# Linear attention feeding a Swish MLP: input weights and first V as fp32 on the hardware DMA queue, cast on chip; first queries issued by two engines

## The chip, the cores and the metric

The kernel runs on one core of a Trainium2 chip. The metric is the device time of one execution in microseconds (us); lower is better. The kernel before took 290.16 us (median of three runs, 289.76 to 290.47). Engines: PE is TensorE's matmuls and PEld its weight loads, DVE is VectorE, ACT is ScalarE, POOL is GpSimd, SP is SyncE. SP, ACT and POOL can all issue DMAs. SP and ACT use the hardware queue (q1 and q10 in the profile), POOL the software queue (q0).

All runs quoted here count as "fast" (none more than 1.5% above the fastest of its kernel), so they can be compared.

## The reference, cut to what matters

```
q, k, v: [8 batches, 8 heads, 576, 64] fp32
q_s = softmax(q, over the 64);  k_s = softmax(k, over the 576)
attn = q_s @ (k_s^T @ v)                      # per batch and head
x = attn as [4608 tokens, 512]
h = x @ w_in                                   # 512 -> 2048
out = (h / (1 + exp(-beta*h))) @ w_out         # 2048 -> 512
```

## The kernel before

The tokens are worked off in nine slabs of 512. Slabs 0 to 7 are the first 512 positions of one batch each; the last slab holds the rests. A slab's pass 1 is `h` for 16 blocks of 128 columns (four matmuls each, then one Swish activation on ACT, which writes `GT`); pass 2 is `@ w_out`. Attention of the next batches is threaded between those matmuls at fixed "slots". Only the first two batches are special: batch 0's attention runs in front (the *head*), and batch 1's is squeezed into slab 0's pass 2, because its inputs have just come. The product `k_s^T @ v` is called the kv product below; a query pair is the queries of two of the eight heads.

The parts that matter here:

```
# batch 0's loads, all issued by SyncE, in this order
load_main("qf", qt_h, QF, 0, 4)        # queries: four loads of 256 KB
load_k(0, 4)                           # K: four loads of 288 KB
... (beta)
# V of batch 0 and the input weights: GpSimd's DMA, which casts fp32 to bf16 on the way
def load_vb(hp):                       # two of these, 0.59 MB read each
    add(POOL, lambda e: e.dma_start(o, a), ..., after=P.writer[("qf", 0, 2)])
def load_win(c):                       # five of these, 4.19 MB read in all
    add(POOL, lambda e: e.dma_start(WIN[:, :, c0:c0 + n], a), ...)
    if c == 2:
        wgate.append(P.ops[-1])        # the output weights may be issued when this has landed
...
load_vb(0)
warm(8, 0)                             # filler matmuls that keep PE busy
exp_q(0); exp_kh(...)                  # ACT: exponentials
norm_main(0, 0, 1)                     # DVE: sum, reciprocal, multiply
norm_main(0, 1, 1, POOL)               # the multiply of query pair 1 on GpSimd
...
# slab 0, pass 2: loads for batch 1 follow the output weights (1 MB each)
for c in range(4): load_wout(c)
...
for cs in ((0, 1), (2, 3)):
    load_main("qf", qt_h, QF, 1, 4, cs)
    load_k(1, 4, cs)
load_v(1, 4)                           # four loads of 288 KB, cast to bf16 by GpSimd
```

The weight columns of block `f` are not neighbours: PE's weight load takes 128 columns with a step of `n`, and the rows of `w_out` are read in the matching order, so that they come in longer pieces. `n` is 2 for `f < 4` and 4 from there on.

The softmax here doesn't subtract the row's maximum and nothing guards it: scores larger than these inputs give would overflow.

## Time and profile before

| what | number | view |
|---|---|---|
| time | 290.16 us, profiled run 290.93 | runs |
| span, PE busy | 289.1 us, 96% | the page |
| dense pass 1 of slab 0 begins | 18.1 to 19.8 us | timeline |
| PE waits for batch 1's V in slab 0 | weight loads 1.3 us, in two waits | waits |
| from slab 1's first activation to the end | 235.92 us | timeline |

The page of the kernel before, its first lines and its chain of waits (part 4, followed back from the last instruction):

```profile
span 289.1 us, 3841 instructions
PE 278.7 (96%) x1566; PEld 137.8 (48%) x1597; DVE 111.4 (39%) x199; ACT 176.8 (61%) x237; POOL 38.1 (13%) x58
...
q1 hardware_dynamic: 37738, 43.92, 50.0%
q0 software_dynamic: 3184, 2.69, 6.3%
...
PE 82%; DMA 7%; SPq 5%; POOL 3%; issue 2%; DVE 0%; POOLq 0%
```

PE is the bottleneck nearly everywhere, so only what makes PE wait can be won. The queue lines give packets and megabytes as they are *written*: the 5.37 MB of fp32 that the software queue read count as 2.69, because it writes bf16.

The timeline of the head (start us, length us, engine, line, operation, output<-input; in brackets the idle time before it and what ended it):

```profile
0.74 2.00 SPq L254 DMA_DIRECT2D QF<-in_q_dram  x4
...
3.43 0.63 ACT L297 ACTIVATE EQ<-QF 128x512 bf16<-128x512 f32 x1 [1.20 <-DMA QF<-in_q_dram]
...
7.77 0.63 ACT L297 ACTIVATE EQ<-QF 128x512 bf16<-128x512 f32 x1 [0.67 <-DMA QF<-in_q_dram]
7.77 1.04 POOL L336 TENSOR_TENSOR EQ<-EQ,QI 128x512 bf16<-128x512 bf16 x1
8.09 1.27 DVE L336 TENSOR_TENSOR EQ<-EQ,QI 128x512 bf16<-128x512 bf16 x1
```

The last of the four query loads is used at 7.77 us. GpSimd's multiply also starts there, beside a VectorE multiply that takes 1.27 us (alone it takes 0.69).

The timeline of slab 0, where batch 1's V comes in:

```profile
44.05 0.88 POOL L353 CAST VB<-VF 128x576 bf16<-128x576 f32 x1 [3.13 <-DMA VF<-in_v_dram]
...
44.98 0.10 PEld L367 LDWEIGHTS PS<-VB,EK 128*128 128x128 bf16 x1 [0.98 <-POOL VB L353]
...
45.14 0.67 POOL L353 CAST VB<-VF 128x576 bf16<-128x576 f32 x1 [0.21 <-DMA VF<-in_v_dram]
...
45.86 0.10 PEld L367 LDWEIGHTS PS<-VB,EK 128*128 128x128 bf16 x1 [0.33 <-POOL VB L353]
...
53.18 1.26 ACT L649 ACTIVATE GT<-PS,BETA 128x512 bf16<-128x512 f32 x2 [0.48 <-PE PS L367]
```

GpSimd waits for a load, PE waits for GpSimd. The last line is slab 1's first activation.

Two stretches in the windows view (stretch, its length, busy us of PE, PEld, DVE, ACT and POOL with instruction counts, granted PE clock, DMA share, GB/s written):

```profile
2.00:6.00 4.00, 2.89 (x9) 0.90 (x8) 1.84 (x4) 1.48 (x4) 2.50 (x5) 1.00 0.95 290
10.00:22.00 12.00, 11.21 (x109) 6.77 (x110) 5.34 (x17) 7.13 (x11) 5.94 (x10) 1.00 1.19 174
```

The first is queries and K on the hardware queue. The second is almost all software queue; 174 GB/s written as bf16 are 348 GB/s read as fp32.

### The profile page before, as it was taken

The page shows a single profiled execution, that of the slowest core. Times are in us where ns is not written, and L with a number is a line of the kernel's source. Part 1 is how long each engine was busy: PE and PEld are TensorE (multiplying, and loading weights), DVE is VectorE, ACT ScalarE, POOL GpSimd, SP SyncE. Part 2 cuts the span into 40 slices and gives each one's busy share as a digit, 9 for nine tenths or more (in the row PEclk, how much of TensorE's full clock was granted, in tenths as well). Part 3 has the DMA queues.
Part 4 walks back from the last instruction along what each step waited for, and adds up shares of the span by engine and source line. Part 5 has one row for each costly group of instructions (what it writes and reads, how often), then busy time and mean ns, then how long its engine had stood idle before and what let it go on. Part 6 is the DMA issues. An engine that isn't in the chain of part 4 may idle for free.

```text
span 289.1 us, 3841 instructions
## 1 busy us (share of the span) xinstructions
PE 278.7 (96%) x1566; PEld 137.8 (48%) x1597; DVE 111.4 (39%) x199; ACT 176.8 (61%) x237; POOL 38.1 (13%) x58
## 2 busy tenths in 40 slices
PE   6899998999999999999999999999999999999994
PEld 2455444454555444544454445544544454445441
DVE  4641667206883147304660555054804300110021
ACT  4748774879987963788378926892660076018500
POOL 5920014022603011300040000000000000000000
PEclk9999999999999999999999999999999999999999
DMA  6999999995699999905990025001800030012022
GB/s 215 198 193 346 405 376 302 356 384 146 162 381 240 347 325 403 126 0 168 384 194 0 2 91 128 2 1 51 170 17 0 0 147 0 0 67 80 0 74 73
DMA packets 41260, 47.38 MB, mean 164 GB/s; under 512 B 20117, under 2 KB 31383, under 8 KB 39834
## 3 DMA queue, kind: packets, MB, share of 16 engines
q1 hardware_dynamic: 37738, 43.92, 50.0%
q0 software_dynamic: 3184, 2.69, 6.3%
q10 hardware_dynamic: 320, 0.52, 0.5%
q8 instruction: 12, 0.20, 0.3%
q14 instruction: 6, 0.05, 0.0%
HBM read 36.71 MB, written 9.44 MB: 160 GB/s over the span
## 4 chain that ended last, share of the span: by engine, by line
PE 82%; DMA 7%; SPq 5%; POOL 3%; issue 2%; DVE 0%; POOLq 0%
PE PS L367 82%; DMA VF<-in_v_dram 4%; DMA WIN<-in_moe_w_in_dram 3%; SPq L254 3%; SPq L264 1%; POOL EK L238 1%; SPq L548 1%; POOL VB L602 1%; POOL WIN L564 1%; POOL EQ L336 0%; DVE O2S L701 0%; POOL VB L353 0%; POOL IDB L226 0%; PE PS L365 0%; POOL KVD L241 0%
## 5 line engine op out<-in xcount | busy, mean ns | idle before, releaser
L649 ACT ACTIVATE GT<-PS,BETA 128x512 bf16<-128x512 f32 x144 | 98.1, 687 | 79.2 <-PE PS L367 79.0
L367 PE MATMUL PS<-WOUT,GT 128*128 128x512 bf16 x562 | 131.8, 379 | 0.6
L367 PE MATMUL PS<-XT,WIN 128*128 128x512 bf16 x561 | 131.1, 380 | 1.0 <-ACT XT L526 0.3
L367 PEld LDWEIGHTS PS<-XT,WIN 128*128 128x128 bf16 x576 | 62.2, 109 | 59.6 <-DVE XT L526 1.5
L367 PEld LDWEIGHTS PS<-WOUT,GT 128*128 128x128 bf16 x576 | 54.5, 98 | 62.1 <-DVE O2S L701 0.2
L701 DVE COPY O2S<-PS 128x512 f32<-128x512 f32 x34 | 23.2, 686 | 110.7 <-PE PS L367 110.7
L367 PE MATMUL PS<-VB,EK 128*128 128x65 bf16 (+1 forms) x288 | 36.6, 198 | 1.1 <-POOL VB L353 0.7
L353 POOL CAST VB<-VF 128x576 bf16<-128x576 f32 x28 | 20.0, 713 | 74.6 <-PE PS L367 60.6
L309 ACT ACTIVATE EK<-KF 64x1152 bf16<-64x1152 f32 x24 | 27.8, 1158 | 0.4
L367 PEld LDWEIGHTS PS<-VB,EK 128*128 128x128 bf16 x288 | 22.8, 102 | 9.0 <-POOL VB L353 1.3
L334 DVE TENSOR_REDUCE QS<-EQ 128x8 f32<-128x512 bf16 (+1 forms) x22 | 20.2, 919 | 3.3 <-ACT EQ L297 3.1
L297 ACT ACTIVATE EQ<-QF 128x512 bf16<-128x512 f32 x32 | 18.0, 620 | 5.2 <-DMA QF<-in_q_dram 5.0
L442 DVE CAST XT<-PS 128x512 bf16<-128x512 f32 x24 | 16.4, 690 | 10.9 <-PE PS L367 10.9
L336 DVE TENSOR_TENSOR EQ<-EQ,QI 128x1024 bf16<-128x1024 bf16 (+1 forms) x16 | 17.4, 1085 | 0.6
L367 PE MATMUL PS<-QT,KVD 128*128 128x512 bf16 x31 | 11.6, 379 | 0.2
L336 POOL TENSOR_TENSOR EQ<-EQ,QI 128x512 bf16<-128x512 bf16 x6 | 6.2, 1040 | 34.2 <-DVE QI L335 33.9
L319 ACT ACTIVATE EK<-KF 64x1152 bf16<-64x1152 f32 (+1 forms) x10 | 9.5, 966 | 1.8 <-DMA KF<-in_k_dram 1.6
L367 PE MATMUL PS<-WARM 128*128 128x512 bf16 x18 | 8.9, 631 | 1.4 <-DVE ONE L223 1.2
L404 DVE TENSOR_TENSOR KVD<-PS,RC 64x128 bf16<-64x128 f32 (+1 forms) x22 | 7.7, 349 | 2.9 <-PE PS L367 2.3
L342 DVE TENSOR_REDUCE QRS<-EQR 128x8 f32<-128x512 bf16 x4 | 2.7, 680 | 14.4 <-ACT EQR L324 14.4
L526 ACT CAST XT<-PS 128x512 bf16<-128x512 f32 x4 | 2.2, 587 | 7.6 <-PE PS L367 7.6
L553 DVE TENSOR_SCALAR WOUT<-WST,RB 128x512 bf16<-128x512 f32 x8 | 3.3, 483 | 8.5 <-DMA WST<-in_moe_w_out_dram 8.5
(48 smaller groups left out, 82.6 us busy)
## 6 DMA issues: line engine op xcount, KB each, us to landing
out_dram<-O2S SPq DMA_DIRECT2D x8, 1024.0 KB, 5.5
KF<-in_k_dram SPq DMA_DIRECT2D x6, 1152.0 KB, 9.6
VF<-in_v_dram SPq DMA_DIRECT2D x6, 1152.0 KB, 11.2
QF<-in_q_dram SPq DMA_DIRECT2D x6, 1024.0 KB, 7.5
KF<-in_k_dram SPq DMA_DIRECT2D x8, 288.0 KB, 7.3
QF<-in_q_dram SPq DMA_DIRECT2D x8, 256.0 KB, 8.8
WST<-in_moe_w_out_dram SPq DMA_DIRECT2D x2, 1024.0 KB, 8.7
O2S<-in_moe_w_out_dram SPq DMA_DIRECT2D x2, 1024.0 KB, 12.7
```

The costliest lines, as they stand in the source:

```text
L254: add(SP, lambda e, c=c: e.dma_start(dst(bufs[i], c * n, n), src(th, b, c * n, n)), w=[(name, i, hp) for hp in range(c * n // 2, (c + 1) * ...
L297: add(ACTE, lambda e, o=o, a=a: e.activation(o, a, ACT.Exp), r=[("qf", i, hp)], w=[("eq", i, hp)])
L309: add(ACTE, lambda e, o=o, a=a: e.activation(o, a, ACT.Exp), r=[("kf", i, h) for h in hps], w=[("ek", i, h, e_) for h in hps])
L319: add(ACTE, lambda e: e.activation(o, a, ACT.Exp), r=[("kf", i, h) for h in hps], w=[("ek", i, h, e_) for h in hps])
L334: add(DVE, lambda e: e.tensor_reduce(s_, a, AX.X, ALU.add), r=ks, w=[("qs", i, hp0)])
L336: add(eng, lambda e: e.tensor_tensor(a, a, vb, ALU.mult), r=ks + [("qi", i, hp0)], w=ks)
L353: add(eng, lambda e: (e.copy if eng == ACTE else e.tensor_copy)(o, a), r=[("vf", i, h) for h in hps] + [("vone", i)], w=[("vb", i, h) for ...
L367: add(PE, lambda e: e.matmul(o, l, r_, start=start, stop=stop), r=r, w=w, bank=[bk])
L404: add(DVE, lambda e, o=o, a=a, s_=s_: e.tensor_tensor(o, a, s_, ALU.mult), r=[("ps", bk)] + [("rc", i, h) for h in hps], w=[("kvd", i, h, ...
L442: add(eng, lambda e: (e.copy if eng == ACTE else e.tensor_copy)(XT[i][:, hp, :], PS[bk][:, :]), r=[("ps", bk)], w=[("xt", i, hp)], bank=[bk])
L649: add(ACTE, lambda e: e.activation(GT[:, f, :], PS[bk][:, :], ACT.Silu, scale=BETA[:, f:f + 1]), r=[("ps", bk), "beta"], w=[("gt", f)], ba ...
L701: add(eng, lambda e: (e.copy if eng == ACTE else e.tensor_copy)(O2S[t % 2][:, u, :], PS[bk][:, :]), r=[("ps", bk)], w=[("o2", t % 2, u)], ...
```

## The change

The intent: no DMA from GpSimd. V of batch 0 and the input weights are loaded as fp32 through SyncE, into buffers that the output weights use later, and cast on GpSimd (V, columns 0 to 511), ScalarE (a quarter of V) and VectorE (columns 512 to 2047). GpSimd is then free sooner. Batch 0's four query loads are issued by SyncE and ScalarE in turn. Along with that, columns 512 to 1023 change their step from 4 to 2, and one group of transposes moves by two slots. The cut diff leaves out what follows from this: batch 0's V gets the padded layout of the other batches with a column of ones, which K's sums now multiply by instead of the constant `ONE`, and the output weights wait for the casts that free their buffers instead of the gate `wgate`.

```diff
-FG = {2: (0, 256), 4: (512, 1024, 1536)}
-WCH = ((0, 256), (256, 256), (512, 512), (1024, 512), (1536, 512))
+FG = {2: (0, 256, 512, 768), 4: (1024, 1536)}
+WCH = ((0, 256), (256, 256), (512, 256), (768, 256), (1024, 512), (1536, 512))
...
-        load_main("qf", qt_h, QF, 0, 4)
+        load_main("qf", qt_h, QF, 0, 4, None, (SP, ACTE))
...
+        load_v(0, 4)
...
         def load_win(c):
-            add(POOL, lambda e, c0=c0, n=n, a=a: e.dma_start(WIN[:, :, c0:c0 + n], a),
-                w=[("win", c)], slot=f"win{c}")
-            if c == 2:
-                wgate.append(P.ops[-1])
+            s = STAGE[c0 // 512][:, :, c0 % 512:c0 % 512 + n]
+            add(SP, lambda e: e.dma_start(s, a), w=ks, slot=f"win{c}")
+        def cast_win(c, m, nm, eng):
+            add(eng, lambda e: e.tensor_copy(WIN[:, x, c0:c0 + n], s), r=ks, ...)
...
-        load_vb(0)
...
+        for hp in range(3):
+            cast_v(0, hp)
+        for m in range(NM):
+            cast_win(0, m, 1, POOL)
+        for m in range(0, NM, 2):
+            cast_win(1, m, 2, POOL)
...
+        cast_v(0, 3, ACTE)
...
-            n = 2 if f < 4 else 4
+            n = 2 if f < 8 else 4
...
-        TT = (104, 119)
+        TT = (106, 119)
...
+        for c in range(2, len(WCH)):
+            for m in range(0, NM, 2 if c < 4 else 1):
+                cast_win(c, m, 2 if c < 4 else 1, DVE)
```

More of the change, by code (lines that the diff above doesn't have):

```diff
@@ L210, in bass_efficient_attn_shen__then__act_swish_beta_kernel @@
         DUMMY = sb("DUMMY", [128, 8], F32)
-        ONE = sb("ONE", [128, 2], BF16)
         PS = [es.enter_context(nc.psum_tensor(f"PS{i}", [128, 512], F32)) for i in range(8)]
@@ L222, in bass_efficient_attn_shen__then__act_swish_beta_kernel @@
         add(DVE, lambda e: e.memset(WARM[:, :], 0.0), w=["warm"])
-        add(DVE, lambda e: e.memset(ONE[:, :], 1.0), w=["one"])
         add(POOL, lambda e: e.iota(IOTA[:, :], [[1, 128]], base=0, channel_multiplier=-1,
@@ L229, in bass_efficient_attn_shen__then__act_swish_beta_kernel @@
             r=["iota"], w=["idf"])
-        def v_ones(i):
-            add(POOL, lambda e: e.memset(VB[i][:, :, :, D:VW], 1.0),
-                w=[("vone", i)] + [("vb", i, hp) for hp in range(NHP)])
         def homes(i):
+            add(POOL, lambda e: e.memset(VB[i][:, :, :, D:VW], 1.0), w=[("vone", i)])
             for e_ in range(2):
@@ L248, in dst, with load_main @@
             return bass.AP(t, h0 * 4 * D, [[H * 4 * D, 128], [4 * D, nh], [1, 4 * D]])
-        def load_main(name, th, bufs, b, split=1, cs=None):
+        def load_main(name, th, bufs, b, split=1, cs=None, engs=(SP,)):
             i = b % 2
@@ L253, in load_main @@
             for c in cs or range(split):
-                add(SP, lambda e, c=c: e.dma_start(dst(bufs[i], c * n, n), src(th, b, c * n, n)),
+                add(engs[c % len(engs)], lambda e, c=c: e.dma_start(dst(bufs[i], c * n, n), src(th, b, c * n, n)),
                     w=[(name, i, hp) for hp in range(c * n // 2, (c + 1) * n // 2)],
@@ L506, in ksum @@
             for j in range(NG):
-                l, _, ke, _, _ = kv_rows(b, hp, j)
-                mm(PS[kb][:, hp:hp + 1], l, ONE[:, 0:1], j == 0, j == NG - 1, r=ke + ["one"],
+                l, r_, ke, kv, ko = kv_rows(b, hp, j)
+                mm(PS[kb][:, hp:hp + 1], l, r_[:, D:D + 1], j == 0, j == NG - 1, r=ke + ko,
                    w=[("ps", kb)], bk=kb)
@@ L517, in kv_mm @@
             for j in range(NG):
-                l, _, ke, kv, _ = kv_rows(b, hp, j)
-                r_ = bass.AP(VB[0], hp * KW + j * D, [[NHP * NG * VW, 128], [1, D]])
-                mm(PS[bk][:, VW * n:VW * n + D], l, r_, j == 0, j == NG - 1,
+                l, r_, ke, kv, ko = kv_rows(b, hp, j)
+                mm(PS[bk][:, VW * n:VW * n + D], l, r_[:, 0:D], j == 0, j == NG - 1,
                    r=ke + kv, w=[("ps", bk)], bk=bk)
@@ L539, in bass_efficient_attn_shen__then__act_swish_beta_kernel @@
                 slot=f"bt{i}")
+        load_v(0, 4)
         STAGE = (WST[0], WST[1], O2S[1], O2S[0])
-        SKEY = ([("wst", 0)], [("wst", 1)], [("o2", 1, u) for u in range(4)],
+        SKEY = ([("wst", 0), ("wst", 2)], [("wst", 1), ("wst", 3)], [("o2", 1, u) for u in range(4)],
                 [("o2", 0, u) for u in range(4)])
         def load_wout(c):
-            n = 2 if c == 0 else 4
+            n = 2 if c < 2 else 4
             a = bass.AP(wout_h, 512 * c * DM, [[n * DM, 128], [128 * n * DM, 4 // n], [1, n * DM]])
@@ L548, in load_wout @@
             add(SP, lambda e: e.dma_start(o, a), w=SKEY[c],
-                slot=f"wst{c}", after=wgate if c == 0 else ())
+                slot=f"wst{c}")
         def scale_wout(c):
@@ L558, in bass_efficient_attn_shen__then__act_swish_beta_kernel @@
         HEAD = (1, 2, 3, 4, 5, 6, 7)
-        wgate = []
         def load_win(c):
@@ L563, in load_win @@
             a = bass.AP(win_h, c0, [[DFF, 128], [128 * DFF, NM], [1, n]])
-            add(POOL, lambda e, c0=c0, n=n, a=a: e.dma_start(WIN[:, :, c0:c0 + n], a),
-                w=[("win", c)], slot=f"win{c}")
-            if c == 2:
-                wgate.append(P.ops[-1])
+            s = STAGE[c0 // 512][:, :, c0 % 512:c0 % 512 + n]
+            ks = SKEY[c // 2][c % 2:c % 2 + 1] if c < 4 else SKEY[c - 2]
+            add(SP, lambda e: e.dma_start(s, a), w=ks, slot=f"win{c}")
+        def cast_win(c, m, nm, eng):
+            c0, n = WCH[c]
+            x = m if nm == 1 else slice(m, m + nm)
+            s = STAGE[c0 // 512][:, x, c0 % 512:c0 % 512 + n]
+            ks = SKEY[c // 2][c % 2:c % 2 + 1] if c < 4 else SKEY[c - 2]
+            add(eng, lambda e: e.tensor_copy(WIN[:, x, c0:c0 + n], s), r=ks,
+                w=[("win", c, y) for y in range(m, m + nm)])
         def turn_beta():
@@ L597, in bass_efficient_attn_shen__then__act_swish_beta_kernel @@
         kb = bank(HEAD)
-        def load_vb(hp):
-            a = bass.AP(vt_h, hp * 2 * HS, [[KW, 128], [2 * HS, 2], [1, KW]])
-            o = bass.AP(VB[0], hp * KW, [[NHP * NG * VW, 128], [KW, 2], [1, KW]])
-            add(POOL, lambda e: e.dma_start(o, a), w=[("vb", 0, hp), ("vb", 0, hp + 1)],
-                slot=f"vb{hp}", after=P.writer[("qf", 0, 2)])
-        load_vb(0)
         warm(8, 0)
@@ L619, in bass_efficient_attn_shen__then__act_swish_beta_kernel @@
         norm_main(0, 3, 1)
-        load_vb(2)
         for c in range(len(WCH)):
             load_win(c)
+        for hp in range(3):
[4 more added lines that the diff above has]
+            cast_win(1, m, 2, POOL)
         homes(1)
-        v_ones(1)
         go(t_steps(0, (1,), HEAD))
@@ L641, in pass1_mm @@
             rd = [("xt8", p_) for p_ in range(4)] if t == 8 else [("xt", t % 2, m)]
-            n = 2 if f < 4 else 4
+            n = 2 if f < 8 else 4
             l = bass.AP(WIN, m * DFF + 128 * (f // n * n) + f % n, [[NM * DFF, 128], [n, 128]])
             mm(PS[bk][:, :], l, x[:, m, :], m == 0, m == NM - 1,
-               r=rd + [("win", c) for c in range(len(WCH))
+               r=rd + [("win", c, m) for c in range(len(WCH))
                        if WCH[c][0] <= 128 * (f // n * n) < WCH[c][0] + WCH[c][1]],
@@ L765, in bass_efficient_attn_shen__then__act_swish_beta_kernel @@
             elif t == 1:
-                v_ones(0)
                 for hp in range(NHP):
```

## The prediction

> **What bounds it now.** The page gives PE 96% of a 289.1 us span; the chain of waits is 82% PE matmuls. By stretch (the windows view), PE is busy 230.9 of the last 236.1 us. So two places can move the time: the head, until the dense pass-1 matmuls begin at 18.1 to 19.8 us (timeline), and the first slab, where the waits view has PE waiting some 1.3 us (44.5 to 46 us) for GpSimd's casts of V of batch 1. Behind those the chain runs over V loads, SyncE issues, and the input-weight load landing at 20.45 us that gates the output-weight loads. DMA share is 1.0 or more from 7 to 53 us: the V wait is a bandwidth wait.
>
> **What the change removes.** Seven GpSimd DMA issues (5.6 us of GpSimd), one of which held up GpSimd's multiply of query pair 1 until 7.77 us, its input ready at 6.58; and 5.37 MB read through the software queue from about 8.9 to 27 us, roughly 295 GB/s. The hardware queue in this trace moved 360 to 395 GB/s for Q, K and V, 430 for output weights. Estimate from these: 5.37 MB takes 14.5 us instead of 18.
>
> **What it adds.** GpSimd: three V casts at 0.67 to 0.88 us, input-weight casts of about 2.7 us by the same rate. ScalarE: one V cast, about 0.6, two query issues at about 0.5. VectorE: 12 casts of 128x512, at most 0.48 each as the output-weight scaling takes, so 4 to 6 us, where it is idle (20.4 to 28.1). The Trainium skill's GPSIMD Engine Reference (Key points) says GpSimd shares its SBUF interfaces with VectorE; this trace agrees: a VectorE multiply beside GpSimd's took 1.27 us, alone 0.69.
>
> **On the critical path.** Head: pair 1's multiply ends about 1 us sooner, pair 2's 0.5. But the K sums need ScalarE's exponentials (fourth K one ends at 11.07 us, sums start at 11.5), which follow K landings at 8.5 to 10.6; those hardly move. V should land at 11.4 to 13.5, casts end by 14.2, first input weights be cast by 16.3, before PE needs them (kv at 14.5, pass 1 at 17.7). Head gain 0.3 to 0.9 us. Issuing queries on two engines alone gains little: the queue was 0.94 busy from 2 us.
> Middle: output weights land 1 us sooner (first near 27 instead of 28.1), V of batch 1 near 42.8 instead of 44.0. PE gets there 0.5 us sooner, so its wait shrinks by about 0.7.
> Sum: about 1.1 us gained. Predicted 289.0 us, range 287.8 to 290.6; faster by over 2%: 1%, within: 95%, slower: 4%.
>
> **What would show it.** First pass-1 matmul near 17.6; no software queue in the DMA table; output weights landing near 27; V of batch 1 near 42.8, PE's wait for its casts under 1 us; the late stretch unchanged. Wrong if PE's wait in the head is for a V or weight cast.
>
> **What would make it wrong.** Staging is used twice: output weights cannot be issued before the input weights in their buffer are cast. If VectorE's casts end later than about 27 us, the queue runs dry and V of batch 1 comes later. Weight rows in 1 KB pieces may run no faster than the 285 to 297 GB/s of the first queries; VectorE casts may be late for input columns 512 to 1023, wanted at 22.5 us; two queues may delay the first query or K. The moved transposes (slot 106) hint that batch 1's queries may come later relative to PE.

## The result, and the profile after

The changed kernel took 289.12 us (median of four runs, 289.09 to 289.28); the kernel before took 289.96 us beside it. The ratio is 0.997, 95% interval 0.9953 to 0.9987. A ratio here is the mean time of one kernel's fast runs over that of the other's in the same rounds, so it is not quite the ratio of the medians. The interval leaves out 1. The predicted number, 289.0, was right within 0.12 us; how much of that was luck is told below.

The profile also looked like the prediction. The page after:

```profile
span 287.3 us, 3906 instructions
PE 279.0 (97%) x1597; PEld 136.0 (47%) x1597; DVE 114.7 (40%) x210; ACT 177.1 (62%) x238; POOL 38.5 (13%) x60
...
q1 hardware_dynamic: 41068, 48.77, 54.3%
q10 hardware_dynamic: 864, 1.05, 1.1%
...
PE 92%; DMA 3%; SPq 2%; POOL 2%; issue 0%; DVE 0%; POOLq 0%
```

The software queue is gone. The head and the place of batch 1's V, timeline:

```profile
0.75 1.04 ACTq L249 DMA_DIRECT2D QF<-in_q_dram  x2
0.75 0.98 SPq L249 DMA_DIRECT2D QF<-in_q_dram  x2
...
4.17 1.15 ACT L292 ACTIVATE EQ<-QF 128x512 bf16<-128x512 f32 x2 [0.85 <-DMA QF<-in_q_dram]
...
5.53 1.15 ACT L292 ACTIVATE EQ<-QF 128x512 bf16<-128x512 f32 x2 [0.21 <-DMA QF<-in_q_dram]
...
7.47 1.04 POOL L331 TENSOR_TENSOR EQ<-EQ,QI 128x512 bf16<-128x512 bf16 x1 [2.52 <-DVE QI L330]
...
8.47 0.69 DVE L331 TENSOR_TENSOR EQ<-EQ,QI 128x512 bf16<-128x512 bf16 x1
...
41.98 0.66 POOL L348 CAST VB<-VF 128x576 bf16<-128x576 f32 x1 [1.40 <-DMA VF<-in_v_dram]
...
43.63 0.10 PEld L362 LDWEIGHTS PS<-VB,EK 128*128 128x128 bf16 x1
...
51.66 0.69 ACT L648 ACTIVATE GT<-PS,BETA 128x512 bf16<-128x512 f32 x1 [0.48 <-PE PS L362]
```

V of batch 1 is cast 2.07 us sooner (41.98 against 44.05), and PE no longer waits for it. Slab 1 begins 1.52 us sooner.

The windows after, same stretches:

```profile
2.00:6.00 4.00, 2.79 (x7) 0.73 (x5) 1.10 (x3) 2.93 (x5) 2.67 (x6) 1.00 0.99 322
10.00:22.00 12.00, 11.48 (x112) 6.51 (x110) 6.60 (x20) 7.18 (x11) 7.93 (x14) 0.77 1.07 371
```

The clock column (1.00 before, 0.77 after, from 10 to 22 us) is not a difference between the kernels. The trace of before holds no clock record until 17.06 us, and the view counts that as 1.00; its filler matmuls at 12.80 and 13.22 us began 0.42 us apart, those of the trace after at 12.41 and 12.84 us 0.43.

It is tempting to stop here. But the two spans differ by 1.8 us where the medians differ by 0.8: the profile of before is of one of its slower runs. A single pair of traces cannot say which of the differences belong to the change. The experiments can.

A caution on the chain of waits. In the trace after, it runs from the input-weight load over GpSimd's casts and a GpSimd memset of `EK` to PE at 19.9 us. That memset clears batch 1's buffer, which those PE matmuls don't read. What they need, the third query-output cast on VectorE, ended at 19.13 us, and PE went on at 19.25. A wait with several semaphores is put down to the one that came last, here the wrong one.

### The profile page after: what moved, and what is told of

It is laid out like the page before. It is cut to its first block, busy times and chain, and to the rows that moved or that the text cites. A ratio compares the mean times of both kernels' runs of the same rounds, so it can differ in the third digit from the quotient of the medians.

```text
span 287.3 us, 3906 instructions
## 1 busy us (share of the span) xinstructions
PE 279.0 (97%) x1597; PEld 136.0 (47%) x1597; DVE 114.7 (40%) x210; ACT 177.1 (62%) x238; POOL 38.5 (13%) x60
## 4 chain that ended last, share of the span: by engine, by line
PE 92%; DMA 3%; SPq 2%; POOL 2%; issue 0%; DVE 0%; POOLq 0%
PE PS L362 91%; DMA WST<-in_moe_w_in_dram 3%; SPq L259 1%; POOL WIN L568 1%; POOL EK L233 1%; SPq L249 0%; PE PS L360 0%; DVE O2S L703 0%; SPq L532 0%; POOL VB L230 0%; POOLq L142 0%
## 5 line engine op out<-in xcount | busy, mean ns | idle before, releaser
L362 PE MATMUL PS<-WOUT,GT 128*128 128x512 bf16 x576 | 133.3, 379 | 0.0
L362 PEld LDWEIGHTS PS<-XT,WIN 128*128 128x128 bf16 x576 | 60.0, 106 | 60.7 <-POOL EK L233 0.7
L362 PE MATMUL PS<-VB,EK 128*128 128x65 bf16 (+2 forms) x324 | 37.1, 193 | 0.0
L348 POOL CAST VB<-VF 128x576 bf16<-128x576 f32 x31 | 22.5, 727 | 75.0 <-DMA VF<-in_v_dram 46.7
L362 PEld LDWEIGHTS PS<-VB,EK 128*128 128x128 bf16 x324 | 23.4, 100 | 8.0 <-issue 1.1
L331 DVE TENSOR_TENSOR EQ<-EQ,QI 128x1024 bf16<-128x1024 bf16 (+1 forms) x16 | 16.6, 1036 | 0.6
```

What stands on the lines that cost most here:

```text
L331: add(eng, lambda e: e.tensor_tensor(a, a, vb, ALU.mult), r=ks + [("qi", i, hp0)], w=ks)
L348: add(eng, lambda e: (e.copy if eng == ACTE else e.tensor_copy)(o, a), r=[("vf", i, h) for h in hps] + [("vone", i)], w=[("vb", i, h) for ...
L362: add(PE, lambda e: e.matmul(o, l, r_, start=start, stop=stop), r=r, w=w, bank=[bk])
```

## The experiments

Twelve kernels ran, each five rounds against the kernel before (six fast runs of each kernel). Each also left one trace, so there are 14 traces with the first two. The landings quoted are the last of a load's 16 completions in the trace's DMA records.

### First call: which part carries the gain?

The theory at this point was the prediction's: the hardware queue brings weights and V sooner, and GpSimd's freed second shortens the head. The rival: the query split does it.

**q_only.** The kernel before, with the split alone.

```diff
-        load_main("qf", qt_h, QF, 0, 4)
+        load_main("qf", qt_h, QF, 0, 4, None, (SP, ACTE))
```

> The kernel before with one part of the change alone: batch 0's query loads issued by SyncE and ScalarE in turn. Main theory (the gain is GpSimd's freed second in the head plus the faster landing of weights and V): this part alone gives nothing, 289.7 to 290.4 us, ratio 0.999 to 1.002; the first query lands later (near 4.1 instead of 3.4 us), the last one earlier (near 6.0 to 6.5 instead of 7.75), and the first dense pass-1 matmul stays within 0.3 us of 19.75. Rival (the query split is what helped): at least half of the measured 0.85 us, so 289.5 us or less.

Measured: 289.34 us (288.67 to 289.79), ratio 0.9978 (0.9948 to 1.0008). The median lies where the rival put it, not where the main theory did. The interval just includes 1.

**no_q.** The changed kernel with the split undone (the reverse of that diff).

> The changed kernel with the query split undone (all four loads from SyncE). Main theory: 288.8 to 289.3 us, the whole gain is kept; the first query lands near 3.4 us again. Rival (query split): it falls back by at least 0.4 us, to 289.5 or more.

Measured: 289.80 us (289.33 to 290.77), ratio 0.9999 (0.9968 to 1.0031). Again the rival's side: with all of the hardware queue and all casts in place, but not the split, the gain is gone.

**w_hw.** The kernel before with the input weights moved as in the change (loads on SyncE, casts, column order), V of batch 0 left on GpSimd's queue, queries left on SyncE.

```diff
-            add(POOL, lambda e, ...: e.dma_start(WIN[:, :, c0:c0 + n], a), ...)
+            add(SP, lambda e: e.dma_start(s, a), ...)      # and cast_win as in the change
```

> The kernel before with only the input weights moved to the hardware queue and cast on GpSimd and VectorE; V of batch 0 stays on GpSimd's DMA queue, queries stay on SyncE. Main theory: the head keeps its length (pair 1's multiply still near 7.8 us, first dense pass-1 matmul near 19.75, perhaps later if V now shares the engines with the weights), but output weights land near 27 to 27.6 us and V of batch 1 near 42, so PE's wait for its casts goes from about 1.3 us to under 0.5: 289.3 to 289.9 us. Rival (only the head counts, or only the query split): 290.0 or more.

Measured: 290.24 us, ratio 1.0008 (0.9978 to 1.0037). A miss for the main theory. The first output weights landed at 28.31 us, not near 27, and V of batch 1 at 43.5; PE's weight loads waited 1.2 us for its casts. In the head PE now also waited 1.5 us for batch 0's V, which shared the engines with the weights, as had been allowed for. So this kernel tells less than it should: it adds a wait of its own.

**mul_first.** The kernel before; GpSimd multiplies first and issues its first V load after that.

```diff
-        load_vb(0)
         warm(8, 0)
...
         norm_main(0, 1, 1, POOL)
+        load_vb(0)
```

> The kernel before with one reordering: GpSimd does pair 1's multiply before it issues the first V load. Main theory (the DMA issue held up the multiply, and the overlap of the two multiplies slowed VectorE): multiply at about 6.6 instead of 7.8 us, VectorE's pair-2 multiply near 0.69 instead of 1.27 us, PE's kv products start 0.3 to 0.5 us sooner unless V, issued a microsecond later, lands too late (its first half landed at 12.4, needed at 14.5); the wait for V of batch 1 then grows by what the head gains, because it is bound by DMA, so the time falls by 0.0 to 0.3 us only: 289.6 to 290.2. Rival (the head alone makes the gain): 289.4 or less.

Measured: 290.11 us, ratio 1.0000 (0.9965 to 1.0034). The mechanism was as expected: GpSimd's multiply at 6.80 us, VectorE's at its full speed (0.69 us), the first kv product at 14.24 instead of 14.93. The time did not move. Input weights then came later, and PE waited 1.6 us for them in slab 0.

### Second call: the method's own noise, and the column order

**before_again** and **after_again** are the two kernels unchanged.

> The kernel before, unchanged: a control for the method and a second trace. Ratio 1.000 within its interval; runs spread over 1 to 3 us. In the trace: the last K chunk of batch 0 lands between 10.2 and 10.7 us, V of batch 1 (first, second quarter) not before 42.8 and 43.9, as in all four traces without the query split (42.8 to 44.0); the stretch from the first activation of slab 1 to the end is 235.9 us, as in all traces of this column order.

> The changed kernel, unchanged: control and second trace, in the same rounds as the kernel before. Ratio 0.995 to 0.999. Query-split theory: last K chunk near 9.2 to 9.7 us, V of batch 1 near 41.9 and 43.0, as in both traces with the split. The stretch from slab 1's first activation to the end 235.65 us.

Measured: before_again 289.64 us (289.07 to 290.71), ratio 0.9982 (0.9954 to 1.0011); after_again 289.05 us (288.89 to 289.75), ratio 0.9959 (0.9936 to 0.9982). Two things follow. First, the same kernel can come out at 0.998 of itself, 0.5 us: differences of that size between two labels say nothing alone. Second, my marker fell. In this trace of the *kernel before*, batch 1's V landed at 41.61 and 42.52 us, sooner than in the changed kernel (41.92 and 43.30). The expectation had said "not before 42.8". The landing at the end of this long queue of loads varies by more than 2 us from run to run.

What separates the two groups in every trace is its beginning. In all seven traces without the split the last query landed between 6.61 and 7.75 us, in all seven with it between 5.69 and 6.02; and from 2 to 6 us the queues wrote 281 to 304 GB/s without, 322 to 336 with. The same window of three more kernels: q_only, no_q2 (the changed kernel without the split) and before_again:

```profile
2.00:6.00 4.00, 2.41 (x7) 0.76 (x5) 1.35 (x3) 2.94 (x5) 2.72 (x6) 1.00 1.04 327
```

```profile
2.00:6.00 4.00, 2.87 (x9) 0.87 (x8) 1.81 (x4) 2.05 (x5) 2.67 (x6) 1.00 0.95 304
```

```profile
2.00:6.00 4.00, 2.66 (x7) 0.73 (x5) 1.63 (x4) 1.67 (x5) 2.51 (x5) 1.00 0.91 288
10.00:22.00 12.00, 11.05 (x110) 6.44 (x112) 4.71 (x16) 6.99 (x11) 5.28 (x9) 0.81 1.24 188
```

A narrower window settles two rivals. From 3.5 to 4.8 us every data packet in all 14 traces is a 1 KB piece of a query: the query issues were over by 2.76 us, and K's first piece (2,304 bytes) started at 4.81 us or later. There the windows view gives 213 to 319 GB/s in the seven traces without the split and 360 to 381 in the seven with it. So in this stretch neither the issue time that SyncE saves nor K's larger pieces make the difference.

The last line shown is the software queue's stretch in before_again: 188 GB/s written, 376 read, against 371 for the hardware queue in the changed kernel. Over all traces with one of the two queues alone in this stretch, the software queue read 348 to 376 GB/s (six traces, mean 363) and the hardware queue 369 to 373 (seven). The two queues deliver nearly the same: by these rates the 5.37 MB take an estimated 14.8 and 14.5 us. The landings agree: from the last K load of batch 0 to column 1535 of the input weights, the same 4.33 MB (V and three quarters of the weights) took 12.3 and 12.4 us in the two traces of before and 12.7 and 12.0 us in the two of the changed kernel.

**fg_only.** The kernel before with the column order alone.

```diff
-FG = {2: (0, 256), 4: (512, 1024, 1536)}
+FG = {2: (0, 256, 512, 768), 4: (1024, 1536)}
-            n = 2 if f < 4 else 4
+            n = 2 if f < 8 else 4
```

> The kernel before with only the column order of weights 512 to 1023 changed from steps of 4 to steps of 2 columns (and the output weights' row order that goes with it). Column-order theory, from the four slabs' rates (257.2 against 254.2 ns per matmul of columns 512 to 1023 in slabs 2 to 6): the stretch from slab 1's first activation to the end is 235.65 instead of 235.92 us, slabs 2 to 6 show 254.2 ns; head and slab 0 as before; in time -0.25 us, which the rounds cannot tell from nothing (289.5 to 290.3). Rival (that stretch differs because of the moved slot or the V layout): it stays 235.9 and 257.2.

Measured: 289.87 us, ratio 0.9981 (0.9954 to 1.0008), as expected not to be told from nothing by the clock. But the trace tells it: the stretch from slab 1's first activation to the end is 235.66 us. That stretch is remarkably steady: 235.92 to 235.95 in the four traces with the old order, 235.64 to 235.67 in the ten with the new one. In slabs 2 to 6 a pass-1 matmul of columns 512 to 1023, with the short kv products that stand between, takes 254.2 instead of 257.2 ns (from the distances of the activations). The page's weight-load line for all pass-1 products has 109 ns per load in before and 106 in fg_only. In slabs 7 and 8, where no kv products stand between, the same columns take 215.8 to 215.9 ns in both orders: the step costs only where the short products are. The start of four activations of slab 2, before:

```profile
85.78 0.69 ACT L649 ACTIVATE GT<-PS,BETA 128x512 bf16<-128x512 f32 x1 [0.34 <-PE PS L367]
86.81 0.69 ACT L649 ACTIVATE GT<-PS,BETA 128x512 bf16<-128x512 f32 x1 [0.34 <-PE PS L367]
87.83 0.69 ACT L649 ACTIVATE GT<-PS,BETA 128x512 bf16<-128x512 f32 x1 [0.34 <-PE PS L367]
88.86 0.69 ACT L649 ACTIVATE GT<-PS,BETA 128x512 bf16<-128x512 f32 x1 [0.34 <-PE PS L367]
```

and in fg_only:

```profile
84.81 0.69 ACT L649 ACTIVATE GT<-PS,BETA 128x512 bf16<-128x512 f32 x1 [0.33 <-PE PS L367]
85.83 0.69 ACT L649 ACTIVATE GT<-PS,BETA 128x512 bf16<-128x512 f32 x1 [0.33 <-PE PS L367]
86.85 0.69 ACT L649 ACTIVATE GT<-PS,BETA 128x512 bf16<-128x512 f32 x1 [0.33 <-PE PS L367]
```

Three distances in the first fence make 3.08 us, two in the second 2.04: about 1.027 against 1.02 us per block. Small, but in every slab from 2 to 6.

**n1.** The changed kernel with step 1 for columns 0 to 1023.

```diff
-FG = {2: (0, 256, 512, 768), 4: (1024, 1536)}
+FG = {1: tuple(range(0, 1024, 128)), 4: (1024, 1536)}
-            n = 2 if f < 8 else 4
+            n = 1 if f < 8 else 4
```

> The changed kernel with columns 0 to 1023 in their natural order (step 1 instead of 2). If the step of the weight load is what costs where short kv products stand between, columns 512 to 1023 fall below 254.2 ns per matmul in slabs 2 to 6 and columns 0 to 511 below 241.3, the stretch from slab 1 to the end by some 0.3 us more, to about 235.3. Against it: output-weight rows are then read in 2 KB instead of 4 KB pieces, which may land them 0.2 to 0.6 us later. Time 288.6 to 289.4. Rival (the step does not matter below 4): 254.2 and 235.65 stay.

Measured: 289.54 us, ratio 0.9969 (0.9945 to 0.9994). The late stretch stayed at 235.65 us and the columns at 254.2 ns: step 4 costs, step 2 does not. The rival holds. The first output weights landed at 28.16 us in this trace, against 27.64 and 27.14 in the changed kernel, as feared, so there was nothing to win here.

### Third call: sufficient, necessary, and what bounds slab 0

**split_fg.** The kernel before with the split and the column order, nothing else.

> The kernel before with two small parts of the change only: the query split and the new column order. Input weights and V stay on GpSimd's DMA queue; no casts on GpSimd, VectorE or ScalarE are added. Theory now: the split is worth about 0.6 us, the order 0.27, the move to the hardware queue nothing, so this has the whole gain: 288.9 to 289.4 us, ratio 0.995 to 0.998, last query of batch 0 near 5.9 us, tail after slab 1's first activation 235.65. The prediction's theory (the hardware queue makes the gain): no more than the column order's 0.3 us, 289.6 or more.

Measured: 289.41 us (288.61 to 290.14), ratio 0.9978 (0.9951 to 1.0005). This is at the edge of what was expected, and three of its six runs were at 289.9 or more. The prediction's theory had put it at 289.6 or more. The point estimate favours the two small parts, but the run does not settle that they have the whole gain. Its trace shows where the software queue can still hurt: the head was short (first activation at 18.25 us, because the full clock came early, at 10.56), and PE's weight loads then waited 2.1 us in slab 0 for input weights, 1.17 of it for columns 512 to 1023 (landed at 20.79; at 17.18 and 18.68 in the changed kernel's first trace).

**no_q2.** no_q once more, under another label.

> The changed kernel with the query split undone, once more, because the first time it was 289.8 us, between the two kernels. Theory now: only the column order is left of the gain, 289.6 to 290.1, ratio 0.998 to 1.001; last query of batch 0 at 6.6 us or later. Rival (the split does nothing): 289.0 to 289.3, as the changed kernel.

Measured: 289.84 us (289.28 to 290.49), ratio 0.9995 (0.9973 to 1.0017). Undoing the split takes the gain away, a second time on another chip. Twelve runs of this kernel average 289.88 us, the ten runs of the changed kernel 289.17: 0.7 us (not all on the same chip; against the kernel before in the same rounds 0.9999 and 0.9995 stand against 0.997 and 0.9959). Both have the new column order, so that is not in this difference.

**v1_late.** The changed kernel with 0.59 MB loaded once more in front of batch 1's V.

```diff
+                load_v(0, 4, (0, 1))
                 load_v(1, 4)
```

> The changed kernel with 0.59 MB loaded once more ahead of batch 1's V (batch 0's first V half, into its own place, unused): at the 370 to 430 GB/s of this stretch V of batch 1 lands 1.4 to 1.6 us later, near 43.4 and 44.7 us. If PE's arrival at V of batch 1 (43.7 to 43.9 in the changed kernel) is what this landing bounds, slab 0 grows by 0.4 to 1.2 us and the time by as much, 289.5 to 290.4; the head and the stretch from slab 1 on stay. If nothing waits for V there, the time stays 289.1.

Measured: 289.65 us (289.42 to 290.21), ratio 0.9992 (0.9971 to 1.0013); the changed kernel had 289.05 and 289.12. V of batch 1 landed at 43.16 and 44.14 us, about 1.2 and 0.8 later than in the changed kernel's first trace, and PE's wait is back:

```profile
43.22 0.66 POOL L348 CAST VB<-VF 128x576 bf16<-128x576 f32 x1 [2.86 <-DMA VF<-in_v_dram]
...
43.93 0.10 PEld L362 LDWEIGHTS PS<-VB,EK 128*128 128x128 bf16 x1 [0.81 <-POOL VB L348]
...
45.01 0.10 PEld L362 LDWEIGHTS PS<-VB,EK 128*128 128x128 bf16 x1 [0.52 <-POOL VB L348]
```

So the landing of batch 1's inputs does bound slab 0, and a landing about a microsecond later costs about half a microsecond of time.

**no_fill.** The changed kernel without the last five filler matmuls before the kv products.

```diff
         ksum_inv(0, kb, 0, 2)
-        warm(3, 0)
...
         cast_v(0, 3, ACTE)
-        warm(2, 0)
```

> The changed kernel without the last five filler matmuls in front of the first kv products (each 0.43 us at the low clock): the head shortens by 1 to 2 us (first activation of slab 0 near 18.2 to 19 instead of 20.2). Theory: batch 1's queries, K and V are bound by DMA, PE comes to them earlier and waits, so slab 0 grows by most of it; time 288.6 to 289.3, a gain of at most 0.5 us. Rival (a shorter head counts in full, as the prediction's sum assumed): 287.2 to 288.2 us.

Measured: 289.01 us (288.47 to 290.10), ratio 0.9973 (0.9949 to 0.9998). Its head and its slab 1, timeline:

```profile
17.23 1.27 ACT L646 ACTIVATE GT<-PS,BETA 128x512 bf16<-128x512 f32 x2 [1.06 <-PE PS L362]
...
52.15 0.69 ACT L646 ACTIVATE GT<-PS,BETA 128x512 bf16<-128x512 f32 x1 [0.48 <-PE PS L362]
```

and the waits of PE's weight loads from 33 to 53 us (who waited for whom: us in total, times, longest):

```profile
PEld PS L360 <- POOL EQ L331: 1.1, 1, 1.1
PEld PS L362 <- DVE KVD L399: 1.0, 1, 1.0
PEld PS L362 <- POOL VB L348: 0.8, 2, 0.5
```

The head is 3.06 us shorter than in the changed kernel (first activation at 17.23 instead of 20.29 us), and slab 1 starts no sooner (52.15; the two traces of the changed kernel have 51.66 and 52.00). It went into waits: these 2.9 us for batch 1's queries, kv and V, and before them 1.5 us, from 22.1 to 23.9, around the casts of input weights that had landed at 22.42. Not all of the 3.06 us comes from the fillers: the full clock came at 9.48 us in this trace, before the first of them, and at 15.54 in the changed kernel's. The rival, that a shorter head counts in full, is refuted. Neither this kernel nor any other here is clearly faster than the changed one.

Over all 14 traces:

| trace | its run, us | slab 0's first activation | V of batch 1, second quarter landed | slab 1's first activation |
|---|---|---|---|---|
| before | 290.93 | 20.77 | 45.09 | 53.18 |
| before_again | 289.36 | 19.72 | 42.52 | 51.64 |
| mul_first | 291.00 | 19.60 | 44.92 | 53.27 |
| fg_only | 288.66 | 19.41 | 43.11 | 51.21 |
| w_hw | 290.64 | 20.85 | 44.87 | 53.20 |
| no_q | 289.51 | 19.79 | 43.87 | 52.07 |
| no_q2 | 289.37 | 20.09 | 43.53 | 51.92 |
| q_only | 289.33 | 19.56 | 42.75 | 51.59 |
| split_fg | 290.13 | 18.25 | 44.18 | 52.66 |
| after | 289.09 | 20.29 | 43.30 | 51.66 |
| after_again | 289.43 | 20.14 | 42.68 | 52.00 |
| n1 | 289.77 | 19.78 | 43.79 | 52.32 |
| v1_late | 289.81 | 19.90 | 44.14 | 52.34 |
| no_fill | 289.62 | 17.23 | 43.01 | 52.15 |

The start of slab 1 goes with the landing of V (correlation 0.89 over the 14) and not with the end of the head (0.18).

## Why the prediction was right or wrong

The number was right, and the bound was right: slab 0 waits for batch 1's inputs, and those are bound by DMA. The reasons given for the gain were mostly wrong; errors cancelled, and that the number came out within 0.12 us was luck.

- **"5.37 MB takes 14.5 us instead of 18" failed.** This was the main term. I had divided the software queue's bytes by its whole lifetime, 8.9 to 27 us, in which the first output weights already shared the engines, and so got 295 GB/s. In the stretch where it was alone it read 348 and 376 GB/s (twice the 174 and 188 written), and the hardware queue then wrote 371. The half of the estimate that was wrong is the 18 us: the moved bytes cost nearly the same on both queues (an estimated 14.8 and 14.5 us). The kernels with the hardware queue but not the split gained nothing (no_q 0.9999, no_q2 0.9995, w_hw 1.0008), although the column order alone should have given them 0.27 us.
- **"Issuing queries on two engines alone gains little" failed.** The gain does not survive without it: undoing it costs 0.7 us. (That it gains as much alone is not shown: q_only's interval includes 1.) I had read the DMA share of 0.94 as "full". It was not: the rate from 2 to 6 us rose from between 281 and 304 GB/s to between 322 and 336. Some 40 GB/s more over 4 us are 0.16 MB, an estimated 0.4 us at the later 370 GB/s; the rest of the 0.7 I cannot account for, and no trace of a slow run without the split was taken. That the head start is handed on through the loads, which keep the queues busy until V of batch 1, is argued from the full DMA share in that stretch and from v1_late, not shown link by link. The means fit it: K's last load landed at 9.5 us with the split (six traces, v1_late left out) and at 10.2 without (seven), the second quarter of batch 1's V at 43.3 and 44.0; but single traces of one kind scatter by up to 2.6 us.
- **"Head gain 0.3 to 0.9 us" was wrong in effect.** mul_first had the predicted sequence (multiply sooner, VectorE at full speed, kv 0.69 us sooner) and gained nothing (with the caveat that its weights then came later); no_fill's head was 3.06 us shorter, and it gained nothing over the changed kernel. Nor did the head get clearly shorter: its end lay at 20.29 and 20.14 us in the two traces of the changed kernel, at 20.77 and 19.72 in the two of before. In a sum of head and slab 0, the head's term is zero as long as slab 0 waits for DMA. Besides, GpSimd's multiply in the changed kernel runs at 7.47 us, later than in before_again (7.11): the split makes the first query land later (the earliest load at 3.9 to 4.2 us in the seven traces with it, 3.4 to 3.7 in the seven without), as two loads now come in together.
- **"PE's wait shrinks by about 0.7"** was the right size (it went from 1.3 to nothing in the two profiles), for the wrong cause, and the pair of profiles flattered it.
- **"Late stretch unchanged" failed.** It is 0.28 us shorter, from the column order, which I read in the diff as bookkeeping for the staging buffers. fg_only shows it alone.
- **The added casts cost nothing,** as predicted: VectorE's twelve casts took 0.36 to 0.50 us each in the first trace (predicted at most 0.48) and lay in idle time; GpSimd's six weight casts took 3.21 us (predicted 2.7).
- **The risks named:** the staging buffers' second use did not hold up the output weights (27.64 us, against 28.11 and 27.25 in the two traces of before).

So the sum reads: query split about 0.7, column order 0.27, hardware queue and casts about nothing, head nothing: about 1.0, where 0.8 and 1.3 us were measured in medians. What stays open is whether the first two alone suffice (q_only and split_fg both gave 0.9978, with intervals that just include 1), or whether the hardware queue helps once the split is there; five rounds cannot tell 0.3 us from nothing here.

## What to carry to other kernels

When a stage waits for the end of a long row of loads, time is won at the row's slowest place, which may be its first few microseconds; a shorter compute head in front of it is given back as waiting. Compare the rate of two queues in a stretch where each is alone, and count the bytes on the same side of a cast. Before explaining a difference of a third of a per cent, take a second trace of the unchanged kernel: here it moved the supposed marker by more than the change did.

## What the Trainium skill lacked or had wrong

- "DMA: Bandwidth & Descriptors", section "Issuing engines are not separate DMA queues": it says that issuing on several engines only saves the sequencer's time to issue. The runs differ: SyncE issued a 256 KB query load every 0.5 us, some 500 GB/s, yet with one issuer the queues wrote 281 to 304 GB/s from 2 to 6 us, with two 322 to 336 (213 to 319 and 360 to 381 from 3.5 to 4.8 us, with all query loads issued). The page has no word on a start-up rate; why a second queue raises it stays open.
- "TensorE: Matmul & The Clock Gate", section "Weight-path perf modes — Fast Weight Load (FWL) and DoubleRow": it allows a wide range of column steps for the weight load and gives no cost for a step. Here a step of 4 bf16 columns cost 3.0 ns per matmul where short products alternate (257.2 against 254.2 ns) and nothing where none do (215.8 to 215.9), and steps of 2 and 1 were equal.
- The same page, section "Part 1: The HAM clock gate", says that the window is free-running and the ramp run-variable. The traces agree and give the size for this kernel: PE's lasting full clock came at 17.1 and 14.6 us in two runs of the kernel before, at 15.5 and 14.9 in two of the changed one, at 10.6 in split_fg and 9.5 in no_fill. The page estimates the cost at under 1% of a typical span. Here an early clock gained nothing visible: in split_fg and no_fill the first activation came at 18.25 and 17.23 us, and slab 1 began at 52.66 and 52.15, no sooner than in the changed kernel (51.66 and 52.00).
- "GPSIMD Engine Reference", section "Key points", on the interfaces shared with VectorE: the traces agree (a VectorE multiply took 1.27 us beside GpSimd's, 0.69 alone); this section gives no size.
